# Attention scores from compact 64x64 query products, with the mask added in PSUM

## The chip, the cores and the metric

The kernel runs on one core of one Trainium2 chip. The metric is the device time of one execution in microseconds (us); lower is better. The core's engines are TensorE (PE in the rows; PEld is its weight loading), VectorE (DVE), ScalarE (ACT), GpSimd (POOL) and SyncE (SP), which here only issues DMAs. Matrix products are written to PSUM, a small memory of 8 banks that PE writes and that VectorE and ScalarE can read; GpSimd and the DMAs work on SBUF.

## What is computed

Three layers follow one another: masked attention, a soft mixture of experts, and a gated feed-forward layer. The change lies in the attention alone:

```python
B, H, S, D = q.shape                      # 4, 8, 576, 64
scores = np.matmul(q, k.transpose(0, 1, 3, 2)) / np.sqrt(D)
rel = pos[:, None] - pos[None, :]
mask_local = (rel >= 0) & (rel < 32)
mask_strided = (rel >= 0) & (pos[None, :] % 32 == pos[:, None] % 32)
# heads 0 to 3 use mask_local, heads 4 to 7 mask_strided
scores = np.where(mask, scores, -1e9)
attn = np.exp(scores - scores.max(-1)); attn /= attn.sum(-1) + 1e-9
x = attn @ v
...
x = moe(x, phi, w1, w2)                   # 8 experts of 4 slots, hidden size 1024
out = feed_forward(x, w_gate, w_val, w_out)
```

## The kernel before

**Attention, in units and steps.** A unit is one head of two batches; there are 16 units. The 576 positions of a strided head are reordered on the host, so that for both kinds of mask a block of 64 queries needs only a band of 96 (local heads, `WID[0]`) or 80 (strided heads, `WID[1]`) keys. A unit has nine such blocks, worked on three at a time: 48 steps `(u, t)`, two local units and two strided units in turn. In each round of the loop at L561 the stages of four neighbouring steps are issued: `expo` of the step before, `qk` of this one, `tr` of the one two back, `pv` of the one three back. Every engine executes its own instructions in the order in which they are issued.

- `qk` (L255): three products (L261), one for each block. The two batches are stacked in the 128 rows of the contraction: `qbd` holds the queries of batch 0 in rows 0 to 63 and those of batch 1 in rows 64 to 127, each against zeros in the other half, so one 128x128 stationary operand gives the scores of both batches. It is read from `qbd` with a stride of nine elements. VectorE then adds the mask and takes the row maximum, block by block, from PSUM to SBUF (L267, with a second instruction that reads the maximum), and multiplies the maxima by -0.125 (L269).
- `expo` (L272): three exponentials on ScalarE (L278) read the masked scores from SBUF.
- `tr` (L281): three transposes on PE (L286) and a copy on ScalarE (L289). `pv` (L292): six products with 64-column stationary operands (L303), one for each block and batch, whose outputs lie in the two halves of a bank; then the normalisation on VectorE (L307 to L309).
- For 24 of the steps `xtr` (L317) follows: three more transposes (L320) and a copy (L321); for every second unit `logits` (L327, product L340). Around two thirds of the stage come `etr` and `slot` (L380, L400, product L405), which already belong to the expert layer.

**Buffers and queues.** The score bank `sc` has two buffers: `qk` of a step waits until the bank of two steps back has been read. `qbd`, `k` and `v` have two buffers each: `load_qk(u + 2)` is issued after the last `qk` of unit `u` (L231 twice, L232), `load_v(u + 2)` after its last `pv` (L241), followed by three GpSimd copies that duplicate a part of `v` (L244). All go through SP's queue, with two to five half-megabyte weight loads for later layers behind them in each unit (`WSCHED`, L177). Parts of a weight conversion (`pre`, L196 to L207) run on VectorE and ScalarE from round 6 on.

**After the attention** come the end of the expert layer's first part, then its two weight products (L598, L686) between 162 and 198 us, then the feed-forward layer (L766 to L835).

Of the kernel before, what the change touches and what calls it, by code (L numbers as in the profile page):

```python
# [9 lines left out]
F32 = mybir.dt.float32  # L10
# [7 lines left out]
S = 576  # L18
HD = 64
# [65 lines left out]
def layout(q, k, v, moe_phi, moe_w1, moe_w2, moe2_w_gate, moe2_w_val, moe2_w_out):  # L85
# [4 lines left out]
    for u, (bp, h) in enumerate(UNITS):  # L90
        y = h // 4
        o = pi if y else np.arange(S)
        qh[u] = q[2 * bp:2 * bp + 2, h][:, o].reshape(2, NT, 64, HD).transpose(0, 3, 2, 1).reshape(2, HD, S)
        kh[u] = k[2 * bp:2 * bp + 2, h][:, o].transpose(0, 2, 1)
        vw[u, ..., :HD] = v[2 * bp:2 * bp + 2, h][:, o].reshape(2, NT, 64, HD).transpose(2, 0, 1, 3)
# [6 lines left out]
    phi = moe_phi.reshape(4, 128, 32).transpose(1, 0, 2).reshape(128, 128)  # L102
    arrs = dict(cst=constants(), phi=phi, qh=qh, kh=kh.reshape(16, 128, S),
                vh=vw.reshape(16, 64, -1),
# [5 lines left out]
def build(ctx: ExitStack, tc: tile.TileContext, cst, phi, qh, kh, vh, w1, w2, wgv, wo, out):  # L110
# [28 lines left out]
    for j in range(AHEAD):  # L139
        qbd.append(lp.tile([128, 2, S], F32, name=f"qbd{j}"))  # L140
        kt.append(lp.tile([128, PAD + S], F32, name=f"k{j}"))
        vt.append(lp.tile([96, 2 * NT * (HD + 1)], F32, name=f"v{j}"))
    col = lp.tile([128, 128], F32, name="col")
    par = lp.tile([128, 16], F32, name="par")
    ml = lp.tile([128, 192], F32, name="ml")
    ms = lp.tile([128, 720], F32, name="ms")

# [79 lines left out]
    def load_qk(u):  # L227
        if u >= 16:
            return
        for b in range(2):  # L230
            SP.dma_start(out=qbd[u % AHEAD][64 * b:64 * b + 64, b, :], in_=qh[u, b])  # L231
        SP.dma_start(out=kt[u % AHEAD][:, PAD:], in_=kh[u])  # L232

    VW = NT * 2 * (HD + 1)
# [13 lines left out]

    def mask(y, i):
        if y:  # L250
            return ms[:, 80 * i:80 * i + 80]
        return ml[:, 96:192] if i else ml[:, 0:96]

    def qk(u, t):
        y = UNITS[u][1] // 4  # L255
        W = WID[y]
        ps = bank("sc", 2)
        for j in range(3):
            i = 3 * t + j
            c0 = 64 * i + SHIFT[y]  # L260
            PE.matmul(out=ps[:, W * j:W * j + W], lhsT=qbd[u % AHEAD].rearrange("p b (m n) -> p n (b m)", n=NT)[:, i, :],  # L261
                      rhs=kt[u % AHEAD][:, c0:c0 + W], start=True, stop=True, skip_group_check=True)
        o = 288 * ((3 * u + t) % 2)
        sm = tmp[:, 576 + o:864 + o].rearrange("p (j k) -> p j k", j=3)
        mx = ap_.tile([128, 8], F32, tag="mx", name="mx", bufs=4)
        for j in range(3):
            DVE.tensor_tensor_reduce(out=sm[:, j, 0:W], in0=ps[:, W * j:W * j + W], in1=mask(y, 3 * t + j), scale=1.0,  # L267
                                     scalar=-3.0e38, op0=ALU.add, op1=ALU.max, accum_out=mx[:, j:j + 1])
        DVE.tensor_scalar_mul(mx[:, 4:7], mx[:, 0:3], -0.125)  # L269
        sc[u, t] = sm, mx  # L270

    def expo(u, t):  # L272
        W = WID[UNITS[u][1] // 4]
        sm, mx = sc.pop((u, t))
        o = 288 * ((3 * u + t) % 2)
        e = tmp[:, o:288 + o].rearrange("p (j k) -> p j k", j=3)
        for j in range(3):
            ACT.activation(out=e[:, j, 0:W], in_=sm[:, j, 0:W], func=AF.Exp, scale=0.125, bias=mx[:, 4 + j:5 + j])  # L278
        ex[u, t] = e
# [197 lines left out]
    with tc.manual_schedule():  # L477
# [3 lines left out]
        for j in range(AHEAD):  # L481
            e = DVE if j == 0 else POOL
            e.memset(kt[j][:, 0:PAD], 0.0)
            for b in range(2):
                e.memset(qbd[j][64 * b:64 * b + 64, 1 - b, :], 0.0)
        for j in range(AHEAD):
# [20 lines left out]
        low(96, 4)  # L507
        cut(ml[:, 0:96], 15, ALU.is_le, h)
        cut(ml[:, 96:192], 3, ALU.is_le, h)
        same(ident, 0, 128)  # L510
# [442 lines left out]
```

## Time and profile before

| | us |
|---|---|
| three runs | 430.12, 422.14, 426.82 (median 426.82) |
| span of the profiled execution | 423.0 |
| attention stage in it, first to last score product | 5.7 to 140.5 |
| expert weights, both products | 162.4 to 198.0 |
| feed-forward layer | 198 to 423 |

The profiled execution has no time of its own beside its span, which runs from its first to its last instruction; the span lies between the lowest run and the median. All durations in the rows come from this one execution. A row of the chain or of the timeline gives a start, a length and a group of instructions of one kind that followed one another; one fp32 matrix product shows as two records of a weight load and a product, one transpose as one.

### The profile page before, as it was taken

The page shows a single profiled execution, that of the slowest core. Times are in us where ns is not written, and L with a number is a line of the kernel's source. Part 1 is how long each engine was busy: PE and PEld are TensorE (multiplying, and loading weights), DVE is VectorE, ACT ScalarE, POOL GpSimd, SP SyncE. Part 2 cuts the span into 40 slices and gives each one's busy share as a digit, 9 for nine tenths or more (in the row PEclk, how much of TensorE's full clock was granted, in tenths as well). Part 3 has the DMA queues.
Part 4 walks back from the last instruction along what each step waited for, and adds up shares of the span by engine and source line. Part 5 has one row for each costly group of instructions (what it writes and reads, how often), then busy time and mean ns, then how long its engine had stood idle before and what let it go on. Part 6 is the DMA issues. An engine that isn't in the chain of part 4 may idle for free.

```text
span 423.0 us, 7338 instructions
## 1 busy us (share of the span) xinstructions
PE 397.1 (94%) x2578; PEld 299.9 (71%) x2578; DVE 270.6 (64%) x832; ACT 199.4 (47%) x465; POOL 137.3 (32%) x142
## 2 busy tenths in 40 slices
PE   9999999999999989999899987698997699999996
PEld 6989888888878755434478665465784488888885
DVE  6767568575543451163799999989996982424432
ACT  3665665755554340033675645364543344444431
POOL 3121112111112100102445454845292656334423
PEclk9999999999995599999999999989898999999999
DMA  7987797798786478999415232223400000202222
GB/s 217 284 254 244 227 239 248 230 315 245 221 225 191 188 280 298 405 407 421 182 36 191 101 100 101 99 103 108 177 11 0 2 0 1 101 0 99 71 81 99
DMA packets 21445, 71.93 MB, mean 170 GB/s; under 512 B 2848, under 2 KB 3232, under 8 KB 19488
## 3 DMA queue, kind: packets, MB, share of 16 engines
q1 hardware_dynamic: 21264, 71.45, 50.1%
q8 instruction: 20, 0.33, 0.3%
q14 instruction: 17, 0.14, 0.1%
q10 hardware_dynamic: 144, 0.01, 0.0%
HBM read 66.73 MB, written 4.72 MB: 169 GB/s over the span
## 4 chain that ended last, share of the span: by engine, by line
PE 75%; DVE 15%; issue 5%; ACT 4%; POOL 0%; DVEq 0%; ACTq 0%
PE o L793 24%; PE sc L261 17%; PE pv L303 6%; PE tr L286 4%; PE pv L686 4%; PE sc L598 3%; DVE h L773 3%; PE tr L320 3%; DVE wg L207 3%; PE gv L766 2%; DVE wg L196 2%; PE gv L767 2%; PE lg L340 2%; DVE wg L203 2%; PE ms L405 1%
## 5 line engine op out<-in xcount | busy, mean ns | idle before, releaser
L775 POOL TENSOR_TENSOR hl<-h,hh 128x512 fp32r<-128x512 f32 (+1 forms) x60 | 79.5, 1326 | 109.2 <-ACT hh L774 109.2
L793 PE MATMUL o<-woh,hh 128*128 128x512 f32 (+1 forms) x222 | 88.7, 401 | 2.9 <-DVE acc L818 2.1
L793 PE MATMUL o<-wol,hh 128*128 128x512 f32 (+1 forms) x222 | 86.9, 394 | 0.0
L261 PEld LDWEIGHTS sc<-k,qbd 128*128 128x128 f32 x288 | 72.3, 333 | 6.9 <-DVE x L309 4.5
L261 PE MATMUL sc<-k,qbd 128*128 128x96 f32 (+1 forms) x288 | 77.0, 408 | 0.0
L774 ACT CAST hh<-h 128x512 fp32r<-128x512 f32 (+1 forms) x60 | 34.7, 578 | 75.3 <-DVE h L773 75.3
L773 DVE TENSOR_TENSOR h<-gv,sg 128x512 f32<-128x512 f32 (+1 forms) x59 | 37.4, 633 | 45.4 <-ACT sg L772 42.0
L793 PE MATMUL o<-woh,hl 128*128 128x512 f32 (+1 forms) x222 | 59.3, 384 | 0.0
L244 POOL COPY v<-v 32x390 f32<-32x390 f32 (+3 forms) x48 | 21.4, 477 | 111.3 <-DMA v<-in_vh 89.1
L793 PEld LDWEIGHTS o<-woh,hh 128*128 128x128 f32 x222 | 43.1, 194 | 14.8 <-DVE acc L818 3.5
L793 PEld LDWEIGHTS o<-wol,hh 128*128 128x128 f32 x222 | 43.2, 195 | 8.6
L278 ACT ACTIVATE tmp<-tmp,mx 128x96 f32<-128x96 f32 (+1 forms) x144 | 42.4, 359 | 11.7 <-DVE mx L269 6.9
L793 PEld LDWEIGHTS o<-woh,hl 128*128 128x128 f32 x222 | 41.5, 189 | 8.6
L772 ACT ACTIVATE sg<-gv 128x512 f32<-128x512 f32 (+1 forms) x60 | 33.4, 557 | 17.6 <-PE gv L766 17.5
L289 ACT COPY tmp<-tr 96x384 f32<-96x384 f32 (+1 forms) x47 | 22.3, 474 | 37.7 <-PE tr L286 37.7
L267 DVE CUSTOM_DVE_ANT_0 tmp<-sc,ms 128x80 f32<-128x80 f32 x72 | 13.6, 238 | 26.6 <-PE sc L261 16.8
L303 PEld LDWEIGHTS pv<-v,tmp 96*64 96x64 f32 (+1 forms) x576 | 23.0, 151 | 10.0 <-issue 8.7
L303 PE MATMUL pv<-v,tmp 96*64 96x65 f32 (+1 forms) x576 | 29.9, 245 | 0.0
L267 DVE CUSTOM_DVE_ANT_0 tmp<-sc,ml 128x96 f32<-128x96 f32 x72 | 14.9, 266 | 19.2 <-PE tr L286 9.6
L766 PE MATMUL gv<-cs,St 128*128 128x512 f32 (+1 forms) x60 | 26.2, 436 | 0.8 <-DVE St L755 0.7
L286 PE MATMUL tr<-cst_t,tmp 128*96 128x128 f32 (+1 forms) x144 | 26.1, 294 | 0.0
L746 PE MATMUL lg<-wg,soT 128*32 128x256 f32 x88 | 11.9, 419 | 14.4 <-DVE wg L207 13.5
(162 smaller groups left out, 567.8 us busy)
## 6 DMA issues: line engine op xcount, KB each, us to landing
w<-in_w SPq DMA_DIRECT2D x56, 512.0 KB, 8.1
g<-in_wgv SPq DMA_DIRECT2D x10, 1024.0 KB, 4.9
g<-in_wo SPq DMA_DIRECT2D x5, 1024.0 KB, 4.8
v<-in_vh SPq DMA_DIRECT2D x16, 292.5 KB, 4.5
qbd<-in_qh SPq DMA_DIRECT2D x32, 144.0 KB, 3.8
k<-in_kh SPq DMA_DIRECT2D x16, 288.0 KB, 3.9
out<-osb SPq DMA_DIRECT2D x17, 256.0 KB, 2.1
wx<-in_w SPq DMA_DIRECT2D x7, 512.0 KB, 5.6
```

Source lines behind the costliest of these rows:

```text
L261: PE.matmul(out=ps[:, W * j:W * j + W], lhsT=qbd[u % AHEAD].rearrange("p b (m n) -> p n (b m)", n=NT)[:, i, :], rhs=kt[u % AHEAD][:, c0:c0 ...
L267: DVE.tensor_tensor_reduce(out=sm[:, j, 0:W], in0=ps[:, W * j:W * j + W], in1=mask(y, 3 * t + j), scale=1.0, scalar=-3.0e38, op0=ALU.add, ...
L278: ACT.activation(out=e[:, j, 0:W], in_=sm[:, j, 0:W], func=AF.Exp, scale=0.125, bias=mx[:, 4 + j:5 + j])
L286: PE.transpose(ps[0:W, 128 * j:128 * j + 128], e[:, j, 0:W], ident)
L289: (DVE.tensor_copy if (u, t) in ATDVE else ACT.copy)(a[0:W], ps[0:W, 0:384].rearrange("p (j q) -> p j q", j=3))
L303: PE.matmul(out=ps[64 * b:64 * b + 64, 65 * j:65 * j + 65], lhsT=a[0:W, j, 64 * b:64 * b + 64], rhs=vt[u % AHEAD][0:W, 65 * (NT * b + 3 * ...
L766: PE.matmul(out=pg[:, 0:n], lhsT=St[f][:, 0:128], rhs=csf[:, t0:t0 + n], start=True, stop=True)
L772: ACT.activation(out=sg[:, 0:n], in_=pg[:, 0:n], func=AF.Silu)
L773: DVE.tensor_tensor(out=h[:, 0:n], in0=pvv[:, 0:n], in1=sg[:, 0:n], op=ALU.mult)
L774: ACT.copy(hh[bi, f][:, 0:n], h[:, 0:n])
L775: POOL.tensor_tensor(out=hl[bi, f][:, 0:n], in0=h[:, 0:n], in1=hh[bi, f][:, 0:n].bitcast(F32), op=ALU.subtract)
L793: PE.matmul(out=o[:, 0:c], lhsT=(a, a, l)[i][:, 128 * t:128 * t + 128], rhs=(woh, wol, woh)[i][f][:, c * k:c * k + c], start=(first and i ...
```

## The change

The queries are laid out compactly: `qbd` (now named `q0`, `q1` in the trace) holds 128 x 576 elements, batch 0 in rows 0 to 63 and batch 1 in rows 64 to 127, with no zeros. One DMA loads it, and one instruction multiplies it by 0.125 in place: on VectorE for unit 0, on GpSimd for the others.

In `qk` two products of a 64x64 bfloat16 identity with a bfloat16 mask (three blocks wide, 288 or 240 columns) first write the mask into PSUM, one for each half; then six 64x64 fp32 products, one for each block and batch, add the scores. The product of batch 0 uses rows 0 to 63 and writes partitions 0 to 63; that of batch 1 uses rows 64 to 127 and writes partitions 64 to 127. One VectorE reduction gives the negated maximum of all three blocks, and the exponentials read PSUM. The score bank is thus read last by ScalarE, no longer by VectorE. The masks are written as bfloat16 and the local mask has four blocks, so that three can be taken in a row.

```diff
-        qh[u] = q[2 * bp:2 * bp + 2, h][:, o].reshape(2, NT, 64, HD).transpose(0, 3, 2, 1).reshape(2, HD, S)
+        qh[u] = q[2 * bp:2 * bp + 2, h][:, o].transpose(0, 2, 1)
...
-        qbd.append(lp.tile([128, 2, S], F32, name=f"qbd{j}"))
+        qbd.append(lp.tile([128, S], F32, name=f"q{j}"))
...
-    ml = lp.tile([128, 192], F32, name="ml")
-    ms = lp.tile([128, 720], F32, name="ms")
+    ml = lp.tile([128, 4, 96], BF16, name="ml")
+    ms = lp.tile([128, 720], BF16, name="ms")
+    idb = lp.tile([128, 64], BF16, name="idb")
...
-        for b in range(2):
-            SP.dma_start(out=qbd[u % AHEAD][64 * b:64 * b + 64, b, :], in_=qh[u, b])
+        t = qbd[u % AHEAD]
+        SP.dma_start(out=t, in_=qh[u])
         SP.dma_start(out=kt[u % AHEAD][:, PAD:], in_=kh[u])
+        (POOL if u else DVE).tensor_scalar(out=t, in0=t, scalar1=0.125, scalar2=1.0, op0=ALU.mult, op1=ALU.mult)
...
         ps = bank("sc", 2)
+        for b in range(2):
+            h = slice(64 * b, 64 * b + 64)
+            PE.matmul(out=ps[h, 0:3 * W], lhsT=idb[h], rhs=mask(y, t)[h], start=True, stop=False, skip_group_check=True)
         for j in range(3):
             i = 3 * t + j
             c0 = 64 * i + SHIFT[y]
-            PE.matmul(out=ps[:, W * j:W * j + W], lhsT=qbd[u % AHEAD].rearrange("p b (m n) -> p n (b m)", n=NT)[:, i, :],
-                      rhs=kt[u % AHEAD][:, c0:c0 + W], start=True, stop=True, skip_group_check=True)
-        o = 288 * ((3 * u + t) % 2)
-        sm = tmp[:, 576 + o:864 + o].rearrange("p (j k) -> p j k", j=3)
-        mx = ap_.tile([128, 8], F32, tag="mx", name="mx", bufs=4)
-        for j in range(3):
-            DVE.tensor_tensor_reduce(out=sm[:, j, 0:W], in0=ps[:, W * j:W * j + W], in1=mask(y, 3 * t + j), scale=1.0,
-                                     scalar=-3.0e38, op0=ALU.add, op1=ALU.max, accum_out=mx[:, j:j + 1])
-        DVE.tensor_scalar_mul(mx[:, 4:7], mx[:, 0:3], -0.125)
-        sc[u, t] = sm, mx
+            for b in range(2):
+                h = slice(64 * b, 64 * b + 64)
+                PE.matmul(out=ps[h, W * j:W * j + W], lhsT=qbd[u % AHEAD][h, 64 * i:64 * i + 64],
+                          rhs=kt[u % AHEAD][h, c0:c0 + W], start=False, stop=True, skip_group_check=True)
+        p3 = ps[:, 0:3 * W].rearrange("p (j k) -> p j k", j=3)
+        mx = ap_.tile([128, 4], F32, tag="mx", name="mx", bufs=4)
+        DVE.tensor_reduce(out=mx[:, 0:3], in_=p3, axis=AX, op=ALU.max, negate=True)
+        sc[u, t] = p3, mx
...
-            ACT.activation(out=e[:, j, 0:W], in_=sm[:, j, 0:W], func=AF.Exp, scale=0.125, bias=mx[:, 4 + j:5 + j])
+            ACT.activation(out=e[:, j, 0:W], in_=p3[:, j], func=AF.Exp, scale=1.0, bias=mx[:, j:j + 1])
...
-            for b in range(2):
-                e.memset(qbd[j][64 * b:64 * b + 64, 1 - b, :], 0.0)
...
         low(96, 4)
-        cut(ml[:, 0:96], 15, ALU.is_le, h)
-        cut(ml[:, 96:192], 3, ALU.is_le, h)
+        same(idb, 3, 64)
+        cut(ml[:, 0], 15, ALU.is_le, h)
+        cut(ml[:, 1:4], 3, ALU.is_le, h.unsqueeze(1).to_broadcast([128, 3, 96]))
```

The places of the order on which the prediction rests are three. On PE, two rounds in the first local units, before; `sc` is the score bank, `tr` the transposes, `pv` the products with `v`:

```order
L261 MATMUL sc<-k_82,qbd_81 128x96 x3
L286 MATMUL tr<-cst_t,tmp 96x128 x3
L303 MATMUL pv<-v_80,tmp 64x65 x6
L261 MATMUL sc<-k_79,qbd_78 128x80 x3
L286 MATMUL tr<-cst_t,tmp 96x128 x3
L303 MATMUL pv<-v_83,tmp 64x65 x6
```

The same two rounds now:

```order
L262 LDWEIGHTS idb
L262 MATMUL sc<-ml,idb 64x288
L262 LDWEIGHTS idb
L262 MATMUL sc<-ml,idb 64x288
L268 MATMUL sc<-k_82,q_81 64x96 x6
L289 MATMUL tr<-cst_t,tmp 96x128 x3
L306 MATMUL pv<-v_80,tmp 64x65 x6
L262 LDWEIGHTS idb
L262 MATMUL sc<-ms,idb 64x240
L262 LDWEIGHTS idb
L262 MATMUL sc<-ms,idb 64x240
L268 MATMUL sc<-k_79,q_78 64x80 x6
```

Three products of 128 columns of weights became two mask products and six score products of 64; `tr` and `pv` stand where they stood.

On VectorE, the start of the program, before; `cst_t`, `ml` and `ms` are the constants and the two masks:

```order
L483 MEMSET k_79 128x32
L485 MEMSET qbd_78 64x576 x2
L504 TENSOR_SCALAR cst_t<-col,par 128x96
L505 TENSOR_TENSOR cst_t<-cst_t,col 128x96
L496 TENSOR_SCALAR ml<-cst_t,par 128x96 x2
L499 TENSOR_SCALAR cst_t<-col,par 128x128
```

And now; `q_78` are the queries of unit 0:

```order
L486 MEMSET k_79 128x32
L234 TENSOR_SCALAR q_78<-q_78 128x576
L505 TENSOR_SCALAR cst_t<-col,par 128x96
L506 TENSOR_TENSOR cst_t<-cst_t,col 128x96
L500 TENSOR_SCALAR idb<-col,par 128x64
L497 TENSOR_SCALAR ml<-cst_t,par 128x96
L497 TENSOR_SCALAR ml<-cst_t,par 128x288
L500 TENSOR_SCALAR cst_t<-col,par 128x128
```

The scaling of the first queries, which needs their DMA, stands ahead of all the masks.

On GpSimd, in the middle of the stage, now (before, the copies of `v` alone stood there):

```order
L234 TENSOR_SCALAR q_78<-q_78 128x576
L246 COPY v_83<-v_83 16x2x130
L246 COPY v_83<-v_83 16x2x195 x2
L234 TENSOR_SCALAR q_81<-q_81 128x576
L246 COPY v_80<-v_80 32x2x130
L246 COPY v_80<-v_80 32x2x195 x2
```

The scaling of the queries of unit `u + 2` stands ahead of the copies of `v` of unit `u + 1`.

## Rows read from the trace of the kernel before

**Rows 1.** The page, part 1: busy us, share of the span and instructions of each engine.
```profile
PE 397.1 (94%) x2578; PEld 299.9 (71%) x2578; DVE 270.6 (64%) x832; ACT 199.4 (47%) x465; POOL 137.3 (32%) x142
```

**Rows 2.** The chain that ended last, 106 to 140 us: start, us, what.
```profile
112.61 0.48 PE tr L320 x3
113.09 1.41 PE sc L261 x6
114.49 0.33 PE tr L286 x3
114.82 0.50 PE pv L303 x12
...
121.66 1.59 PE sc L261 x6
...
128.05 1.33 PE sc L261 x6
129.38 0.64 PE tr L286 x3
130.02 0.85 PE pv L303 x12
130.87 0.83 PE tr L320 x3
```

**Rows 3.** Stretches: length, busy PE, PEld, DVE, ACT, POOL, PE clock, DMA share, GB/s.
```profile
5.90:119.40 113.50, 112.82 (x1011) 97.41 (x1010) 73.02 (x442) 67.29 (x196) 19.54 (x43) 1.00 0.83 251
119.40:143.40 24.00, 24.00 (x171) 19.64 (x173) 10.18 (x71) 10.44 (x31) 2.90 (x7) 0.61 0.71 225
...
162.40:198.00 35.60, 35.26 (x303) 14.87 (x302) 10.87 (x32) 6.70 (x12) 2.02 (x1) 1.00 1.00 391
```

**Rows 4.** The whole chain that ended last: three longer pieces.
```profile
31.02 1.59 PE sc L261 x6
...
47.63 1.60 PE sc L261 x6
...
93.33 1.31 PE ms L405 x24
...
359.42 2.72 PE o L793 x12
```

**Rows 5.** Timeline, 17.4 to 22.9 us: start, us, engine, instruction.
```profile
17.42 1.51 PEld L261 LDWEIGHTS sc<-k,qbd 128*128 128x128 f32 x6
...
19.34 0.43 PEld L303 LDWEIGHTS pv<-v,tmp 96*64 96x64 f32 x12 [0.18 <-issue]
...
20.40 0.85 ACT L278 ACTIVATE tmp<-tmp,mx 128x80 f32<-128x80 f32 x3
```

**Rows 6.** Groups by line and form: busy, mean ns, idle before.
```profile
L775 POOL TENSOR_TENSOR hl<-h,hh 128x512 fp32r<-128x512 f32 x48 | 69.0, 1439 | 90.0 <-ACT hh L774 90.0
...
L485 POOL MEMSET qbd<- 64x576 f32 x2 | 1.1, 572 | 0.1
...
L347 DVE TENSOR_REDUCE nm<-lg 128x1 f32<-128x288 f32 x2 | 0.9, 458 | 3.9 <-PE lg L340 3.9
```

**Rows 7.** Timeline of the start, 0 to 7.5 us.
```profile
0.73 1.21 SPq L231 DMA_DIRECT2D qbd<-in_qh  x2
...
4.19 1.63 DVE L496 TENSOR_SCALAR ms<-cst_t,par 128x80 f32<-128x80 f32 x9
...
5.74 1.94 PE L261 MATMUL sc<-k,qbd 128*128 128x96 f32 x8
...
7.24 0.26 DVE L267 CUSTOM_DVE_ANT_0 tmp<-sc,ml 128x96 f32<-128x96 f32 x1 [1.42 <-PE sc L261]
```

**Rows 8.** The page, part 6: issues, KB each, us to landing.
```profile
w<-in_w SPq DMA_DIRECT2D x56, 512.0 KB, 8.1
...
qbd<-in_qh SPq DMA_DIRECT2D x32, 144.0 KB, 3.8
```

More of the change, by code (lines that the diff above doesn't have):

```diff
@@ L102, in layout @@
     phi = moe_phi.reshape(4, 128, 32).transpose(1, 0, 2).reshape(128, 128)
-    arrs = dict(cst=constants(), phi=phi, qh=qh, kh=kh.reshape(16, 128, S),
+    arrs = dict(cst=constants(), phi=phi, qh=qh.reshape(16, 128, S), kh=kh.reshape(16, 128, S),
                 vh=vw.reshape(16, 64, -1),
@@ L247, in build, with mask @@
     tmp = ap_.tile([128, 1920], F32, name="tmp")
-    def mask(y, i):
+    def mask(y, t):
         if y:
-            return ms[:, 80 * i:80 * i + 80]
-        return ml[:, 96:192] if i else ml[:, 0:96]
+            return ms[:, 240 * t:240 * t + 240]
+        return (ml[:, 1:4] if t else ml[:, 0:3]).rearrange("p a k -> p (a k)")
     def qk(u, t):
@@ L260, in qk @@
             c0 = 64 * i + SHIFT[y]
-            PE.matmul(out=ps[:, W * j:W * j + W], lhsT=qbd[u % AHEAD].rearrange("p b (m n) -> p n (b m)", n=NT)[:, i, :],
-                      rhs=kt[u % AHEAD][:, c0:c0 + W], start=True, stop=True, skip_group_check=True)
-        o = 288 * ((3 * u + t) % 2)
-        sm = tmp[:, 576 + o:864 + o].rearrange("p (j k) -> p j k", j=3)
-        mx = ap_.tile([128, 8], F32, tag="mx", name="mx", bufs=4)
-        for j in range(3):
-            DVE.tensor_tensor_reduce(out=sm[:, j, 0:W], in0=ps[:, W * j:W * j + W], in1=mask(y, 3 * t + j), scale=1.0,
-                                     scalar=-3.0e38, op0=ALU.add, op1=ALU.max, accum_out=mx[:, j:j + 1])
-        DVE.tensor_scalar_mul(mx[:, 4:7], mx[:, 0:3], -0.125)
-        sc[u, t] = sm, mx
+            for b in range(2):
[6 more added lines that the diff above has]
+        sc[u, t] = p3, mx
     def expo(u, t):
         W = WID[UNITS[u][1] // 4]
-        sm, mx = sc.pop((u, t))
+        p3, mx = sc.pop((u, t))
         o = 288 * ((3 * u + t) % 2)
```

## The prediction

> **What bounds the kernel now.** I read the page first, then the chain that ended last, then the stretches, then the timeline of single steps. The page says that PE is busy for 94% of the span and the other engines for at most 64% [rows 1]. The stretches show where this change can act: from 5.9 to 119.4 us PE is busy for 112.8 of 113.5 us while VectorE has 73.0 and ScalarE 67.3 [rows 3]. The chain agrees: through the attention it consists of PE pieces laid end to end, in each step the scores (`sc`), the transposes (`tr`), the products with `v` (`pv`) and, in 24 of the 48 steps, the transposes of `x` (`xtr`) [rows 2]. So a microsecond taken from PE in a step is a microsecond of the stage until another engine or the DMAs become late. A step costs 1.59 + 0.33 + 0.50 = 2.42 us without `xtr` and 1.41 + 0.33 + 0.50 + 0.48 = 2.72 with it [rows 2]; the pattern of two units, six steps with three `xtr` and one `logits`, takes 47.63 - 31.02 = 16.61 us [rows 4].
>
> Two readings of these pieces carry the sum. First, the score piece takes 1.41 us behind `xtr`, which uses all 128 columns of the array as it does, but 1.59 behind `pv`, which uses 64; I take the difference, 0.18 us, as the price of a switch of shape. The gap of 0.18 us ahead of the first weight load of `pv` is the same thing at the other change of shape [rows 5]. Second, what fills the scores is not the columns that stream. Their six weight loads follow one another every 0.25 us [rows 5], and the piece is the same whether 80 or 96 columns stream (1.59 at 31.02, a strided unit; 1.60 at 47.63, a local one [rows 4]). Products with 64 columns of weights show what streaming costs: 24 records of 128 columns, two halves side by side, take 1.31 us, so 0.109 for a pair, or 0.00085 us a column [rows 4].
>
> The Trainium skill (TensorEngine Tiling (Array Packing), Key Properties) says that a change of tiling mode, as against a change of tile, drains TensorE. The 0.18 us agrees with it; the rule speaks against this change, since the scores now have a shape that neither neighbour has.
>
> **The change part by part.** *Scores on PE.* If the two halves run side by side as the halves of `pv` do, a step has six pairs of passes: 6 x 96 x 0.00085 = 0.49 us for local heads, 0.41 for strided ones. No row shows a 64-row bfloat16 product; the nearest rows are the one-pass products of 512 columns, twelve in 2.72 us, 0.227 each [rows 4], which gives 0.13 us for 288 columns and 0.11 for 240, once for both halves side by side (if each took its own turn, twice that). With the switch of 0.18 the score piece becomes 0.80 or 0.70 us; mean 0.75.
>
> *Switches.* Behind `pv` the switch was there already. New are one from the scores to `tr` in all 48 steps, and one from `xtr` to the scores in 24, already counted in the 0.75. So a step without `xtr` goes by 0.75 + 0.18 - 1.59 = -0.66 us, one with it by 0.75 + 0.18 - 1.41 = -0.48. Over 24 of each: -15.8 - 11.5 = -27.3 us. If the switch into `tr` were hidden, 8.6 more would go; if it cost twice as much, 8.6 less.
>
> *VectorE.* Three mask additions with their maximum reads and the scaling of the maxima become one reduction of 288 elements. A reduction of 288 from PSUM takes 0.458 us [rows 6], with one output instead of three; nothing shows the three-output form. VectorE had 73.0 us of work in a stretch that would shrink to about 113.5 x (16.61 - 3.42) / 16.61 = 90 us, so it fits even if the reduction saved nothing. I count no gain and no cost.
>
> *ScalarE.* The exponentials read PSUM instead of SBUF. Three from SBUF take 0.85 us [rows 5]; none from PSUM is in the rows. Even 0.2 us more for each step (some 8 us) would leave 75 us in 90, and less is possible as well; either is covered by PE.
>
> *The bank.* `qk` of step n now waits for the exponentials of step n-2, not for VectorE's reading. Queued behind it on PE stand `tr` and `pv` of the same round, so a late bank delays all of them. After the product come the reduction (0.46), the exponentials (0.85), hand-offs and whatever VectorE and ScalarE still have ahead of them, perhaps 0.8 together: 2.1 us. Available are two steps less one score piece, 2 x 1.76 - 0.75 = 2.8. That is hidden with 0.7 us to spare; if 0.3 us of it failed in each step it would cost 14 us.
>
> *Queries.* One DMA replaces two of the same bytes, which saves SP an issue. The scaling is new: 15 times on GpSimd for 128x576. Its nearest rows are a fill of 64x576 at 0.57 us and a two-input operation of 128x512 at 1.44, or 1.62 for 576 [rows 6]; I take 0.8, nearer to the fill because there is one input. GpSimd has 19.5 us of work in 113.5 [rows 3]. Behind the scaling in its queue wait the copies of `v` of the unit before, whose DMA lands later than the queries anyway.
>
> *The start.* VectorE scales the first queries ahead of all masks. They are issued at 0.73 us [rows 7] and land after some 3.8 [rows 8], at 4.5. The scaling (about 0.5) and five mask operations follow, then the rest of the masks (nine take 1.63 us [rows 7]), before the first maximum: about 9 us where VectorE read the first scores at 7.24. PE has other steps queued, so I take 1.4 us, between 0.5 and 2.5.
>
> *DMAs.* They moved 251 GB/s at a share of 0.83 [rows 3]. The same bytes need 113.5 x 0.83 = 94 us of engine time if packets stay as slow, and 113.5 x 251 / 391 = 73 us at the rate of the saturated stretch. Against 90 us of PE work I take 2 us of stalls, between 0 and 6.
>
> *After the stage.* The weight stretch from 162.4 to 198.0 is bound by the DMAs (share 1.00 [rows 3]), but its loads are released by buffers that PE frees, so it moves forward whole.
>
> *Sum.* -27.3 + 1.4 + 2.0 = -23.9. The profiled execution also lost some 4 us to the lower clock late in the stage: the granted clock is 0.61 in the mean of 119.4 to 143.4 [rows 3], that is, mostly at 1.2 instead of 2.4 GHz, and steps with `xtr` took 3.65 us there against 2.72 [rows 2]. Whether that returns I can't tell; half of it, -1.9, is counted. 423.0 - 25.8 = 397.2; the span lies 3.8 us below the median of the runs (426.82), of which I add one: **398 us**.
>
> **The rivals.** *The loads become late* (408 us). A unit shrinks from 8.3 to about 6.6 us while its queries are requested behind a megabyte of weights that takes 8.1 us to land [rows 8]. With 1.7 us less time to drain, queries land after 5.5 instead of 3.8, and the scaling adds 0.6 to 1.6: 6.1 to 7.1, and they are needed three steps, 6.6 us, after the request. Half a microsecond or so in each of 16 units, some 10 us, goes back. For it: 94 us of DMA time against 90 of PE. Against it: the DMAs reach 391 GB/s elsewhere.
>
> *The halves don't run side by side* (425 us). No row shows two products that use different rows of the array at once; those of `pv` share their rows and differ in columns. In turn the scores cost 0.18 + 0.26 + 0.98 = 1.42 us (local) or 0.18 + 0.21 + 0.82 = 1.21; with the new switch a step goes by 1.31 + 0.18 - 1.59 = -0.10 or, with `xtr`, +0.08. That cancels, and the start makes it slower by about 1.4. The Trainium skill (TensorEngine Tiling (Array Packing), Gotcha 1: PSUM Pressure) states that different row tiles can't access one PSUM bank at the same time, and here both write one bank, if in different partitions; by that rule it would come out so. Rows of `pv` show two tiles sharing a bank in different partitions, which speaks against it.
>
> *The lower clock spreads* (441 us, slower). The new step is made of streaming, which the clock stretches: `pv` takes 0.85 instead of 0.50 [rows 2], 1.7 times. Before, the scores hardly grew (1.33 against 1.41), because their weight loads set the pace. A new step of 1.75 us would take some 3.0, one with `xtr` 1.6 more than at full clock: 1.45 in the mean. From 17 of 48 steps on this eats the gain of 25 us, from 23 on it is over 2% slower; with 30 it costs 43. For it: the clock fell in this very stage with PE never idle. Against it: it held for the first 113 us, and PE's steps hold more streaming per microsecond than before.
>
> **How the numbers follow.** The forecast has 0.60, late loads 0.17, halves in turn 0.17, lower clock 0.06. The forecast's own range is 386 to 408 (switch, start, stalls and clock at their ends). The range for 8 in 10 is 386 to 422: forecast and late loads, and the better part of halves in turn. 2%, about 8.5 us, is what a measurement of this kernel can tell. Faster by more: 0.60 + 0.17 + 0.02 = 0.79; slower by more: 0.06; within: 0.15.
>
> **What would show it.** Right: a score piece near 0.75 us in the chain, its six pairs of starts a few nanoseconds apart; `tr` pieces near 0.5; six steps in about 13.2 us; expert weights starting some 24 us earlier. Pairs 0.08 us apart mean halves in turn; PE waiting for GpSimd's scaling or for `k` means late loads; score products waiting for ScalarE mean the bank. I am wrong if the chain through the stage leaves PE for more than a tenth of it.

## The result, and the profile after

| | before | after |
|---|---|---|
| median | 426.84 us (422.14 to 430.12) | 397.72 us (395.62 to 400.09, 4 runs) |
| span of the profiled execution | 423.0 | 395.6 |
| start of the first step to start of the last in it | 5.7 to 139.2 | 6.3 to 111.2 |
| start of the expert weights | 162.4 | 131.0 |

The ratio is 0.9333, with a 95% interval of 0.9264 to 0.9401: faster, by 29 us in the medians. Forecast were 398 us. In 34 further executions of the kernel before, the time follows the mean granted clock (on one chip 419.52 us at 0.984 and 440.12 at 0.895); at 0.960 to 0.972, about where the changed kernel's executions lie (0.961 to 0.969), it is 422.28 to 424.33 us, so some 25 of the 29 us are the change's and the rest is clock. The attention stage became 28.6 us shorter (133.5 to 104.9); what follows it kept its length (283.8 and 284.4 us).

The page, part 1, of the changed kernel, which answers to [rows 1]:

```profile
PE 365.4 (92%) x2962; PEld 257.8 (65%) x2962; DVE 254.3 (64%) x544; ACT 192.7 (49%) x465; POOL 146.3 (37%) x155
```

PE lost 31.7 us of busy time (397.1 to 365.4). VectorE lost a third of its instructions (832 to 544) and 16 us; GpSimd gained 9. The chain that ended last, 30 to 44 us (start, us, what), answers to [rows 2, 4]:

```profile
30.69 0.22 PE sc L262 x2
30.91 0.41 PE sc L268 x12
31.33 0.45 PE tr L289 x3
31.78 0.50 PE pv L306 x12
32.28 0.24 PE sc L262 x2
32.52 0.49 PE sc L268 x12
...
36.14 0.24 PE sc L262 x2
36.38 0.49 PE sc L268 x12
36.88 0.46 PE tr L289 x3
37.34 0.50 PE pv L306 x12
37.84 0.48 PE tr L323 x3
...
43.39 0.24 PE sc L262 x2
```

L262 is the mask product, L268 the scores. A score piece is now 0.24 + 0.49 = 0.73 us for local heads and 0.22 + 0.41 = 0.63 for strided ones, where 1.59 or 1.41 stood. The transposes behind it grew from 0.33 to 0.46, `pv` (0.50) and `xtr` (0.48) stayed. Twelve records of 96 columns in 0.49 us are six pairs of 0.082 us each, the pace that `pv`-like pairs gave [rows 4]: the two halves run side by side. In the trace the second of a pair mostly starts 3 or 4 ns behind the first.

The same chain, 8 to 70 us, has two pieces that were not there before:

```profile
17.70 7.84 DMA v<-in_vh
...
50.43 7.05 DMA v<-in_vh
```

In both places PE caught up with a transfer of `v`; before, no DMA stood in the stage's chain. The first of them belongs to a unit whose keys were late as well, and whose queries were scaled only at 23.6 us, just when PE came to them. SP requests the queries at 16.77 us and the keys behind them, and PE waits first for the keys, then for `v` (timelines of SP and PE):

```profile
16.77 0.33 SPq L232 DMA_DIRECT2D q<-in_qh  x1
...
24.21 0.63 PE L268 MATMUL sc<-k,q 64*64 64x80 f32 x12 [0.60 <-DMA k<-in_kh]
...
25.59 0.34 PE L306 MATMUL pv<-v,tmp 80*64 80x65 f32 x4 [0.28 <-DMA v<-in_vh]
```

The stretches show busier DMAs (length, busy PE, PEld, DVE, ACT, POOL, clock, DMA share, GB/s; [rows 3]):

```profile
6.40:111.80 105.40, 100.97 (x1542) 73.61 (x1540) 67.54 (x229) 69.51 (x223) 32.05 (x63) 0.97 0.92 298
111.80:131.00 19.20, 16.96 (x193) 11.42 (x191) 10.24 (x40) 6.42 (x19) 1.61 (x3) 1.00 0.89 340
131.00:166.00 35.00, 34.66 (x297) 14.40 (x297) 10.37 (x30) 6.10 (x11) 2.02 (x1) 1.00 1.01 389
```

In the stage the DMA share went from 0.83 to 0.92 and the rate from 251 to 298 GB/s, and PE idles for 4.4 of 105.4 us where it idled for 0.7 of 113.5. Of these 4.4 us, 2.1 are at the start and 1.0 at 72 and 75 us, where it waits for ScalarE; 1.3 are loads (0.6 for `k`, 0.3 for `v`, 0.4 for GpSimd's copies of `v`). The expert weights (third line) moved forward whole, at the same length and rate.

VectorE at the start of the changed kernel (timeline: start, us, instruction, idle before; [rows 7]):

```profile
3.77 0.46 DVE L234 TENSOR_SCALAR q<-q 128x576 f32<-128x576 f32 x1 [2.73 <-DMA q<-in_qh]
...
6.15 2.44 DVE L497 TENSOR_SCALAR ms<-cst_t,par 128x80 bf16<-128x80 f32 x9
8.51 0.81 DVE L272 TENSOR_REDUCE mx<-sc 128x3 f32<-128x288 f32 x2
```

The first maximum comes at 8.5 us, not 7.24. The nine masks of the strided heads start at 6.15 us instead of 4.19 and take 2.44 us, not 1.63. The shortest, median and longest of the nine (ns), after and before, and GpSimd's copies of `v`:

```profile
L497 DVE TENSOR_SCALAR ms<-cst_t,par x9: 254/255/548, 6.1 to 8.0; 128x80 bf16<-128x80 f32 x9
L496 DVE TENSOR_SCALAR ms<-cst_t,par x9: 256/256/262, 4.2 to 5.6; 128x80 f32<-128x80 f32 x9
7.17 1.36 POOL L246 COPY v<-v 32x260 f32<-32x260 f32 x3 [5.76 <-DMA v<-in_vh]
```

A mask written as bfloat16 takes as long as one written as float32: six of the nine take 0.25 us and start every 0.17 us, as all nine did before. The last three take 0.48 to 0.55 us, each about as long as the GpSimd copy that runs beside it; before, the masks were done ahead of these copies. PE issued two score pieces at 6.4 and 7.1 us and its third only at 10.0.

### The profile page after: what moved, and what is told of

Its sections match the earlier page's. It is cut to its first block, busy times and chain, and to the rows that moved or that the text cites. A ratio compares the mean times of both kernels' runs of the same rounds, so it can differ in the third digit from the quotient of the medians.

```text
span 395.6 us, 7785 instructions
## 1 busy us (share of the span) xinstructions
PE 365.4 (92%) x2962; PEld 257.8 (65%) x2962; DVE 254.3 (64%) x544; ACT 192.7 (49%) x465; POOL 146.3 (37%) x155
## 4 chain that ended last, share of the span: by engine, by line
PE 64%; DVE 19%; issue 6%; ACT 5%; DMA 5%; POOL 0%; DVEq 0%; ACTq 0%; POOLq 0%; SPq 0%
PE o L795 24%; PE pv L306 5%; PE tr L289 5%; PE sc L268 5%; PE pv L688 4%; DVE h L775 4%; DMA v<-in_vh 4%; PE sc L600 4%; DVE wg L197 3%; DVE wg L208 3%; PE gv L768 2%; PE tr L323 2%; PE sc L262 2%; DVE wg L204 2%; PE gv L769 2%
## 5 line engine op out<-in xcount | busy, mean ns | idle before, releaser
L795 PE MATMUL o<-wol,hh 128*128 128x512 f32 (+1 forms) x222 | 87.8, 397 | 0.0
L281 ACT ACTIVATE tmp<-sc,mx 128x96 f32<-128x96 f32 (+1 forms) x144 | 37.4, 335 | 6.9 <-DVE mx L272 6.5
L268 PE MATMUL sc<-k,q 64*64 64x96 f32 (+1 forms) x576 | 31.1, 243 | 0.6 <-DMA k<-in_kh 0.6
L272 DVE TENSOR_REDUCE mx<-sc 128x3 f32<-128x288 f32 (+1 forms) x48 | 20.5, 430 | 16.2 <-PE sc L268 11.0
L306 PE MATMUL pv<-v,tmp 96*64 96x65 f32 (+1 forms) x576 | 28.1, 232 | 0.8 <-POOL v L246 0.4
L268 PEld LDWEIGHTS sc<-k,q 64*64 64x64 f32 x576 | 27.9, 138 | 0.8 <-POOL q L234 0.8
L306 PEld LDWEIGHTS pv<-v,tmp 96*64 96x64 f32 (+1 forms) x576 | 21.2, 138 | 10.3 <-issue 7.3
L234 POOL TENSOR_SCALAR q<-q 128x576 f32<-128x576 f32 x15 | 10.1, 671 | 46.3 <-DMA q<-in_qh 25.0
L748 PE MATMUL lg<-wg,soT 128*32 128x256 f32 x88 | 13.8, 465 | 13.6 <-DVE wg L208 12.4
```

What stands on the lines that cost most here:

```text
L268: PE.matmul(out=ps[h, W * j:W * j + W], lhsT=qbd[u % AHEAD][h, 64 * i:64 * i + 64], rhs=kt[u % AHEAD][h, c0:c0 + W], start=False, stop=Tru ...
L281: ACT.activation(out=e[:, j, 0:W], in_=p3[:, j], func=AF.Exp, scale=1.0, bias=mx[:, j:j + 1])
L306: PE.matmul(out=ps[64 * b:64 * b + 64, 65 * j:65 * j + 65], lhsT=a[0:W, j, 64 * b:64 * b + 64], rhs=vt[u % AHEAD][0:W, 65 * (NT * b + 3 * ...
L795: PE.matmul(out=o[:, 0:c], lhsT=(a, a, l)[i][:, 128 * t:128 * t + 128], rhs=(woh, wol, woh)[i][f][:, c * k:c * k + c], start=(first and i ...
```

## The experiments

Three questions were left by the result. Which part of the change brings the time: the 64x64 shape, the contiguous queries that come with it, or the mask in PSUM? What did the start and the late loads cost? And what became of the lower clock? Unless another is named, edits start from the changed kernel. "Last step" is the time at which the last step's score products start in the profiled execution, a measure of the stage: 139.2 us before, 111.3 in the changed kernel.

### Compact queries alone

The kernel before, with the compact `q` and six 64x64 products; masks and maxima stay on VectorE, the scale in the exponentials.

```diff
-            PE.matmul(out=ps[:, W * j:W * j + W], lhsT=qbd[u % AHEAD].rearrange("p b (m n) -> p n (b m)", n=NT)[:, i, :],
-                      rhs=kt[u % AHEAD][:, c0:c0 + W], start=True, stop=True, skip_group_check=True)
+            for b in range(2):
+                h = slice(64 * b, 64 * b + 64)
+                PE.matmul(out=ps[h, W * j:W * j + W], lhsT=qbd[u % AHEAD][h, 64 * i:64 * i + 64],
+                          rhs=kt[u % AHEAD][h, c0:c0 + W], start=True, stop=True, skip_group_check=True)
```

> The compact queries alone: six 64x64 products in a step, but the mask is added and the maximum taken by VectorE block by block as before, no mask product, no scaling on GpSimd, exponentials from SBUF. Theory A (the score products on TensorE carry the gain): the score piece of the chain falls from 1.59 to about 0.6 us, less than in the changed kernel (0.73), and VectorE, with 0.77 us more a step than there is now, becomes the engine without gaps; the stage still shortens by more than 20 us, time 395 to 405. Theory B (the mask in PSUM and the single maximum carry it): the stage keeps most of its 133 us, time above 415.

391.38 us (389.87 to 393.26), ratio 0.9206 (0.9113 to 0.9299): the whole gain and some 6 us more, below what either theory gave. At the same mean granted clock, 0.969, the difference is 2.4 us (393.26 against 395.62). Its chain, 40 to 50 us:

```profile
42.77 0.56 PE sc L262 x12
43.33 0.46 PE tr L287 x3
43.79 0.50 PE pv L304 x12
```

Steps without `xtr` take 1.60 or 1.52 us, 0.08 to 0.09 less than with the mask product. The last step is at 106.2 us. The mask in PSUM thus brings nothing that the compact queries don't bring alone.

### The mask in PSUM alone

The kernel before, with the mask product (128 wide), one maximum, exponentials from PSUM and scaled queries; queries stay zero-padded and strided.

```diff
+        PE.matmul(out=ps[:, 0:3 * W], lhsT=idb, rhs=mask(y, t), start=True, stop=False, skip_group_check=True)
...
-                      rhs=kt[u % AHEAD][:, c0:c0 + W], start=True, stop=True, skip_group_check=True)
+                      rhs=kt[u % AHEAD][:, c0:c0 + W], start=False, stop=True, skip_group_check=True)
```

> The other part alone: zero-padded queries read with a stride of nine elements as before, in three 128x128 products, but the mask comes from one 128x128 bfloat16 product, with one maximum for three blocks and exponentials from PSUM. Theory A: TensorE gets one product of about 0.13 to 0.25 us more in each of 48 steps and nothing less, so 6 to 12 us slower than before, 429 to 438. Theory B: VectorE's shorter path shortens the stage, under 410.

424.36 us in one run, at a mean granted clock of 0.976. The kernel before took 420.05 to 423.43 us on this chip at 0.972 to 0.975, so nothing was gained; rather some us were lost, as theory A says, if fewer. The last step is at 141.4 us, later than the 139.2 of before, which contain half clock. The chain, 40 to 50 us, `pv` ahead of the first mask product and `xtr` ahead of the second:

```profile
40.00 0.24 PE pv L305 x9
40.24 0.23 PE sc L263
40.47 1.38 PE sc L267 x6
...
43.15 0.12 PE sc L263
43.27 1.39 PE sc L267 x6
```

Six strided weight loads still fill 1.38 us. The mask product takes 0.12 us behind `xtr`, whose shape is the same, and 0.23 behind `pv`, so a switch costs 0.11 here. Taking the masks off VectorE gives nothing: its work lay beside PE's.

### Contiguous, zero-padded queries

The kernel before, with 128x128 stationary operands as before, but laid out block by block: GpSimd copies the queries from a staging buffer `qs` between the zeros (the masks as bfloat16, to make room).

```diff
-            PE.matmul(out=ps[:, W * j:W * j + W], lhsT=qbd[u % AHEAD].rearrange("p b (m n) -> p n (b m)", n=NT)[:, i, :],
+            PE.matmul(out=ps[:, W * j:W * j + W], lhsT=qbd[u % AHEAD][:, i].rearrange("p b m -> p (b m)"),
```

> The kernel before with the zero-padded 128x128 weights laid out without a stride (one DMA into a staging tile, two copies on GpSimd, VectorE for unit 0); masks in bfloat16 on VectorE as before. If the stride set the pace of the weight loads (0.25 us each), the loads fall to about 0.11 to 0.16 us, the score piece from 1.59 to 0.9 to 1.2, and 15 to 25 us of the gain come without 64x64 products: 400 to 410. If the width of 128 columns and the two fp32 passes set it, the piece stays above 1.4 and the time within 5 us of before.

394.31 us in one run, with the products of before. The chain, 40 to 50 us:

```profile
42.75 0.82 PE sc L264 x6
43.57 0.33 PE tr L289 x3
43.90 0.50 PE pv L306 x12
...
46.53 0.63 PE sc L264 x6
```

The score piece falls from 1.59 to 0.82 behind `pv` and from 1.41 to 0.63 behind `xtr`, and `tr` keeps its 0.33 since the shape doesn't change. A step of 1.67 us (local) or 1.65 (strided) is as short as the changed kernel's 1.69 and 1.60, though in this run PE also waits 2.9 us for GpSimd's copies of the queries. The stride alone made the score pieces long; the 64x64 shape is one way to be rid of it.

### Compact products with strided queries

The counterpart: the old order of the queries, so that a 64-column operand is read with a stride of nine.

```diff
-                PE.matmul(out=ps[h, W * j:W * j + W], lhsT=qbd[u % AHEAD][h, 64 * i:64 * i + 64],
+                PE.matmul(out=ps[h, W * j:W * j + W], lhsT=qbd[u % AHEAD].rearrange("p (m n) -> p n m", n=NT)[h, i, :],
```

> The changed kernel with the queries in the old order, so that the 64-column weights are read with a stride of nine elements. If a strided load costs about 0.002 us a column (0.25 for 128), 64 columns take 0.125 us against 0.08 of streaming in a pair: pairs of passes would start every 0.125 to 0.25 us instead of 0.083 and the score piece grows by 0.25 to 1.0 us, 410 to 440. If loads of the two halves hide behind the other half's stream, the time stays within 5 us of the changed kernel.

402.49 us in one run, 4.8 more than the changed kernel: within the 5 us of the second expectation, but the loads are not hidden. The chain, 40 to 50 us, a local and a strided step:

```profile
42.00 0.24 PE sc L262 x2
42.24 0.69 PE sc L268 x12
...
48.11 0.22 PE sc L262 x2
48.33 0.69 PE sc L268 x12
```

The scores take 0.69 us whether 96 or 80 columns stream, so the loads set the pace again, but at half the columns they cost 0.20 to 0.28 a step over the contiguous ones. The last step comes at 116.4 us instead of 111.3.

### Batch by batch

```diff
-        for j in range(3):
-            i = 3 * t + j
-            c0 = 64 * i + SHIFT[y]
-            for b in range(2):
+        for b in range(2):
+            for j in range(3):
+                i = 3 * t + j
+                c0 = 64 * i + SHIFT[y]
```

> The changed kernel with the three products of batch 0 issued before the three of batch 1, so that neighbours in the queue no longer lie in opposite halves of the array. If the gain needs the two halves side by side and the queue is followed in order, most passes of a half follow one another alone: the score products take up to twice their 0.49 and 0.41 us, 0.2 to 0.45 us more a step, 407 to 420. If the order of issue doesn't matter, within 3 us of the changed kernel.

422.66 us in one run; almost the whole gain is lost. Stretches of it (columns as above), then two score pieces of its chain, 55 to 76 us:

```profile
11.40:66.00 54.60, 54.60 (x456) 40.55 (x454) 21.08 (x70) 21.98 (x69) 9.68 (x18) 0.50 0.55 174
66.00:112.00 46.00, 45.21 (x649) 34.04 (x648) 30.60 (x98) 29.55 (x94) 12.47 (x23) 1.00 0.93 293
```

```profile
56.21 1.34 PE sc L268 x12
57.55 0.80 PE tr L289 x3
58.35 0.85 PE pv L306 x12
...
67.41 0.61 PE sc L268 x12
```

Two things happened. At full clock the six products of a strided step take 0.61 us, between the 0.41 of alternating halves and twice that: three products of one half behind one another overlap only partly with those of the other. And for 54.6 us, right after the start, the granted clock was at half, 1.2 GHz, with PE never idle; `tr` and `pv` took 1.7 times as long (0.80 and 0.85 us). The last step came at 138.8 us, 27.5 later: 14 steps at half clock took 52.9 us instead of 31.3, and each later one 0.2 us more. By these 0.2 us the order alone would cost some 10 us in 48 steps, an estimate. This is one execution; whether the order brought the clock down or it fell by itself stays open.

### The scale in the exponentials

The scaling of the queries is left to the exponentials, with one small VectorE operation for the maxima.

```diff
-        (POOL if u else DVE).tensor_scalar(out=t, in0=t, scalar1=0.125, scalar2=1.0, op0=ALU.mult, op1=ALU.mult)
...
+        DVE.tensor_scalar_mul(mx[:, 0:3], mx[:, 4:7], 0.125)
...
-            ACT.activation(out=e[:, j, 0:W], in_=p3[:, j], func=AF.Exp, scale=1.0, bias=mx[:, j:j + 1])
+            ACT.activation(out=e[:, j, 0:W], in_=p3[:, j], func=AF.Exp, scale=0.125, bias=mx[:, j:j + 1])
```

> The changed kernel without the scaling of the queries: the factor 0.125 goes back into the exponential, and VectorE multiplies the three maxima by it, one small instruction a step as before. If GpSimd's scaling delays the queries and the start, 2 to 4 us faster than the changed kernel, about 394, with the first products before 6.0 us; if the scaling is hidden, the extra VectorE instruction (about 0.17 to 0.2 us in the chain product, maximum, exponential) leaves it the same within 2 us.

397.64 us (396.54 to 398.83), the same as the changed kernel, and at like mean clocks (0.961 to 0.970). Over the whole run the scaling on GpSimd is hidden.

### Fewer weights in the first units

One half-megabyte weight load less behind each of the units 1 to 3, the three made up later, here on the changed kernel; the same on compact queries alone.

```diff
-WSCHED = [2, 2, 2, 2, 2, 2, 2, 2, 2, 2, 5, 3, 2, 2, 1, 2, 3]
+WSCHED = [2, 1, 1, 1, 2, 2, 2, 2, 2, 2, 5, 3, 3, 3, 2, 2, 3]
```

> The changed kernel with the same thinner weight loads at the start. If late loads are its remaining loss, the stalls around 20 to 28 and 57 us go, and with them the fall of the clock near 27 us: 393 to 395. If TensorE's steps are the bound, within 1 us of 397.7.

> The compact queries alone (VectorE adds the mask), with one half-megabyte weight load less after each of the first three units and the same loads made up in four later units. If late loads of v hold that kernel (stalls of about 4 us between 17 and 32 us), the stalls there shrink and 2 to 4 us go: 387 to 390. If the loads are merely moved and the DMAs are the bound for the whole stage, the stalls come back later and the time stays at 391.

393.40 us (391.59 to 394.23) on the changed kernel, 4.3 less in the medians: the three long steps between 21 and 31 us (2.83, 3.12 and 3.41 us) fell to 2.07, 2.07 and 2.21, a spell of half clock from 26.7 us on was gone with them, and the last step came at 109.1 us, 2.2 earlier. The mean granted clock was higher as well (0.969 to 0.982); at 0.969 the gain is 1.4 us (394.23 against 395.62). So about 2 of the 4.3 us lie in the stage, and the rest comes with the higher clock.

On compact queries alone the four runs took 386.59, 389.86, 392.24 and, at a mean clock of 0.948, 398.42 us. At 0.982 it is 389.86 with fewer weights and 389.87 without: no gain. The profiled execution is the one of 398.42, with 31 us of half clock in and just behind the stage, so little can be read from its steps.

### The mask product twice

```diff
             PE.matmul(out=ps[h, 0:3 * W], lhsT=idb[h], rhs=mask(y, t)[h], start=True, stop=False, skip_group_check=True)
+            PE.matmul(out=ps[h, 0:3 * W], lhsT=idb[h], rhs=mask(y, t)[h], start=False, stop=False, skip_group_check=True)
```

> The changed kernel with the pair of mask products issued twice in every step (the second adds to the first, so that masked scores carry the mask twice; the result of the exponentials is the same). It measures the mask product by doubling it. Theory A (the mask half of the change costs PE time on the path: in the chains the score piece is 0.73 us with it and 0.64 without): another 0.24 us in each of 48 steps, with no further change of shape, so a score piece of 0.96, regular steps of 1.93 and 2.40, less the 3 to 4 us of waits for late loads that the slower steps would cover; 11.5 - 3.5 = 8 us slower than the changed kernel, about 406 us. Theory B (the mask product is hidden, for instance under the weight loads or the loads from memory, and the 6 us between the changed kernel and the one with compact queries alone come from the start): within 2 us of 398. By A the mask product as the change has it costs between 0.06 (what it adds to a switch) and 0.24 us a step, 3 to 11 us.

397.19 us (394.57 to 398.35): the median did not change, as theory B says. But these executions had a higher mean granted clock, 0.970 to 0.981, than those of the changed kernel. The one at 0.970 took 398.35 us, against 395.62 at 0.969, so the second pair does cost time, some 3 us by this one comparison, between the two theories. The chain, 34 to 62 us, shows it (L263) on the path:

```profile
41.64 0.24 PE sc L262 x2
41.88 0.12 PE sc L263 x2
42.01 0.49 PE sc L269 x12
```

It takes 0.12 us (0.10 for strided heads), so the first pair's 0.24 is 0.12 of streaming and 0.12 of switch. Steps grew by 0.1, yet the last step came only 1.4 us later (112.7 us): the thirteenth score piece came 3.0 us earlier than in the changed kernel, which had waited for loads and fallen to half clock by then (29.4 against 32.4 us). Here no half clock fell into the stage, and PE waited 0.7 us for loads, not 1.3.

### The first queries on GpSimd

```diff
-        (POOL if u else DVE).tensor_scalar(out=t, in0=t, scalar1=0.125, scalar2=1.0, op0=ALU.mult, op1=ALU.mult)
+        POOL.tensor_scalar(out=t, in0=t, scalar1=0.125, scalar2=1.0, op0=ALU.mult, op1=ALU.mult)
```

> The changed kernel with the scaling of the first queries on GpSimd instead of VectorE, so that VectorE writes all masks without waiting for the queries' DMA. Theory A (the start costs what the first maximum is late): VectorE's first reduction comes at 7 to 8 us instead of 9 to 10, the third score piece follows 1 to 2 us earlier, and the time falls by about as much, to 396 to 397 us. Theory B (the start is hidden, since PE has steps in the queue and the loads are late anyway a few units on): within 1 us of 398.

Two runs took 400.17 and 400.81 us at a mean granted clock of 0.961 and 0.962, the others 395.71 and 392.79 at 0.970 and 0.978: at 0.961 the changed kernel took 397.33 and 400.09, at 0.969 395.62, so nothing was gained. The first maximum didn't come earlier. VectorE at its start:

```profile
3.97 0.53 DVE L505 TENSOR_SCALAR cst_t<-col,par 128x96 f32<-128x96 f32 x1 [2.93 <-DMA par<-in_cst]
...
6.40 2.45 DVE L497 TENSOR_SCALAR ms<-cst_t,par 128x80 bf16<-128x80 f32 x9
8.77 0.80 DVE L272 TENSOR_REDUCE mx<-sc 128x3 f32<-128x288 f32 x2
```

Without the scaling VectorE waits until 3.97 us for `par`, the constants of the masks. The premise of theory A, that the masks waited for the queries, was wrong. Here, too, masks that lie beside GpSimd's work are the long ones.

The same execution shows what the scaling can cost. The queries requested at 17.05 us landed 8 us later, and PE waited 2.0 us at 25.9 for them to be scaled (GpSimd's timeline):

```profile
25.16 0.67 POOL L234 TENSOR_SCALAR q<-q 128x576 f32<-128x576 f32 x1 [9.99 <-DMA q<-in_qh]
```

### Both corrections, and the masks later

> Both corrections of the changed kernel's known losses together: one weight load less in each of units 1 to 3 (393.4 us alone) and the scaling of the first queries on GpSimd. Theory A (the two losses lie at different places, so they add up): 391 to 392.5 us, level with compact queries alone (391). Theory B (what remains is the mask product's PE time and the start is hidden): 393 to 394 us.

Fewer weights with the first queries on GpSimd: 393.32 us (392.78 to 394.83), as fewer weights alone; theory B. In its profile PE waits 1.6 us at 105 us for late queries to be scaled.

For the last run, on fewer weights, the nine masks of the strided heads are written behind the first maxima:

```diff
-        low(80, 5)
-        for i in range(NT):
-            cut(ms[:, 80 * i:80 * i + 80], 6 + i, ALU.is_lt, h[:, 0:80])
...
+        for t in range(3):
+            late.setdefault(1 + t, []).append((cut_ms, (t,)))
```

> The changed kernel with one weight load less in each of units 1 to 3 (393.4 us alone, third score piece at 10.0 us), and the nine bfloat16 masks of the strided heads, 2.44 us on VectorE ahead of its first maximum, written three by three in rounds 1 to 3 instead; they are needed from round 6 on. Theory A (the start is late because the nine masks, each 0.27 us as bfloat16 against 0.18 before, stand ahead of the first maximum): VectorE's first reduction comes at about 6.7 instead of 8.5 us, the third score piece at 8.2 instead of 10.0, the last score product some 1.5 to 2 us earlier (107 to 107.5), 391.5 to 392 us. Theory B (the start is hidden because something else is late anyway, the loads or VectorE's queue in the rounds that now hold the masks): the third score piece is early but the steps behind it are longer, the last score product stays at 109, 393 to 394 us.

390.48 us (388.28 to 391.57, 6 runs), ratio 0.9266 (0.9202 to 0.9331): 2.9 less in the medians than fewer weights alone and 7.2 less than the changed kernel, at mean granted clocks of 0.978 to 0.987. It is level with compact queries alone: at 0.982 it takes 388.28 to 390.97 us, compact queries 389.87. VectorE at its start:

```profile
6.32 0.46 DVE L272 TENSOR_REDUCE mx<-sc 128x3 f32<-128x288 f32 x1 [0.70 <-PE sc L268]
...
8.16 1.02 DVE L497 TENSOR_SCALAR ms<-cst_t,par 128x80 bf16<-128x80 f32 x3
```

The first maximum is at 6.3 us, the third score piece at 7.8, the last step at 107.2, 1.9 earlier than with fewer weights alone. Some of the start came back as longer steps (2.70 us): two of the masks, now beside GpSimd's copies and a fill, took 2.3 and 2.0 us.

## Why the prediction was right

**Time and place.** 397.72 against 398.0, and the steps named beforehand are in the trace: score pieces of 0.73 and 0.63, starts of a pair a few nanoseconds apart, `tr` near 0.5, six steps in 12.70 us (13.2 forecast), expert weights 31 us earlier (24 forecast). One test it failed: the chain leaves PE for more than a tenth of the stage, with `v` alone. The test was badly chosen, since the chain counts a whole transfer of 7.8 us, most of which lay beside PE's work; PE idled for 4.4 us in all. The rival of halves in turn falls with the 0.49 us for twelve records. By the rule of the Trainium skill (TensorEngine Tiling (Array Packing), Gotcha 1: PSUM Pressure) the two row tiles could not have written one bank at the same time; the trace differs: they did, into different partitions.

**The steps of PE** gained more than forecast. Streaming was right, for scores (0.49 and 0.41) and mask (0.12 and 0.10 against 0.13 and 0.11). The switch was taken at 0.18 us; it measures 0.12 ahead of the mask product and 0.46 - 0.33 = 0.13 into `tr`. That the change of shape has a price agrees with the Trainium skill (TensorEngine Tiling (Array Packing), Key Properties). Six local steps went from 16.61 to 12.70 us, six strided ones from 15.96 to 11.73: four of each make 32.6 us gone in 48 steps, 0.68 a step, not 27.3.

**What was given back** was more, too. The 47 steps between the first and the last should have gained 31.9 us, and the half clock of before 4.1 more (below); the stage shrank by 28.6. So 7.4 us were given back, where 1.4 for the start and 2.0 for late loads were forecast. 6.6 of them went before the twelfth score piece, at which the changed kernel was only 0.3 us ahead (30.62 against 30.95 us).

*Late loads* were put at 2 us, between 0 and 6. Three weight loads less brought the last step 2.2 us forward, so the size was about right. That rival was right in its mechanism as well: in one unit the keys, requested with the queries, came 0.60 us late, then `v`, and with the first queries on GpSimd it was the scaling that PE waited for, 2.0 us. But this befell one or two units of an execution, not all 16, so its 10 us were not lost. *The start* was put at 1.4, between 0.5 and 2.5. Its moment was right (about 9 us forecast, 8.5 measured), its size too small: moving the masks alone brought the last step 1.9 us forward. Its reason was wrong: not the scaling ahead of the masks, but the constants `par`, which land 3.2 us after their issue where it was 1.6 before, and three masks that run beside GpSimd's copies. Why the constants land later is not shown.

Some 4.6 us more from PE's steps and 2.2 more from the clock stand against 4.0 us more given back in the stage and 1.1 ahead of it and behind it. That the median came within 0.3 us of the forecast is therefore luck in part; the spans differ by 1.6 (397.2 forecast, 395.6 measured).

**The lower clock.** Of some 4 us lost to it, half was counted as returning. The profiled execution of before had 14.4 us of half clock up to its last step: four steps took 15.2 us there, 11.1 at full clock, so 4.1 were lost (and 9.5 us of half clock followed). The changed kernel's had two spells of 3.4 us, the second in a step of 3.49 instead of 2.21 us. Ten of the twelve later profiles had 0 to 10.2 us in the stage; the others are batch by batch and compact queries with fewer weights. The rival of a spreading clock did not come, but batch by batch shows that its price was real. What brings the clock down stays open.

**Covered work.** A reduction of 288 takes 0.45 us (0.458 forecast), three exponentials from PSUM 0.81 (0.85 from SBUF [rows 5]), a scaling on GpSimd 0.67 (0.8); none is in the chain of the regular steps. Waiting for the bank shows at the start, where the third mask product follows the exponentials, and once at 71.3 us, behind exponentials of the expert layer.

**What the prediction did not separate.** It read the 0.25 us weight loads as the price of 128 columns of weights, which 64 columns end. The contiguous run shows that the same 128 columns cost less than half of that without the stride (0.63 us for six). The sum holds, since the change removes both, but the 64x64 shape is not what it needed, and it pays two switches a step. The mask half was costed at 0.12 us a step with nothing in return, and that is what it is: alone it brings no gain, and left out it gives 391.38. Part of these 6 us goes with the clock: 2.4 are left at 0.969, and 3.8 between the means if 0.01 of mean clock is worth 2.3 us, as in the kernel before (an estimate from its 20.6 us over 0.089). The second mask product, 0.1 us a step in the chain, cost some 3 us at like clock, so what is left is of the size of a mask product; how much of it is start and loads is not settled. With start and loads mended the mask in PSUM reaches 390.48, level with compact queries alone.

## What to carry to other kernels

When a matmul piece doesn't follow the streamed columns, look at how its stationary operand lies in memory before changing the shape: a strided fp32 operand alone held these pieces at twice their length. A step shortened by 30% moves the bound within a few steps to the next late transfer, so plan the loads anew together with the change. And separate the halves of a change that does two things: here one carried the time and the other none. Before reading a difference of a few us between two versions, set side by side executions with the same granted clock: here two executions of one kernel on one chip lay 20.6 us apart, with 0.089 between their mean clocks.

## What the runs showed of the hardware that was not expected

- Loads of 128 columns of fp32 weights with a stride of nine elements followed one another every 0.24 us, six in 1.38 to 1.41; with the same columns contiguous they came every 0.11 us, and the whole score piece ran in 0.63.
- Products on rows 0 to 63 and on rows 64 to 127 wrote different partitions of one bank side by side: six pairs in 0.49 us. Issued alternately they overlapped fully, three and three only in part (0.61 us instead of 0.41).
- A switch of shape cost 0.11 to 0.19 us, by what stands on either side: 0.11 into a bfloat16 mask product, 0.13 into the transposes, 0.19 into fp32 products.
- A mask operation on VectorE from SBUF to SBUF took 0.25 us alone, with a float32 or a bfloat16 output, and 0.48 to 0.55 beside a GpSimd copy that takes as long (0.43 to 0.52); in the last run two took 2.3 and 2.0 us beside GpSimd's copies and a fill. Reductions that read PSUM kept their 0.44 to 0.46 us beside GpSimd's work.
- On one chip the kernel before took 419.52 us at a mean granted clock of 0.984 and 440.12 at 0.895. In the batch-by-batch run the clock was at half for 54.6 us in which PE never idled.
